# The states' second layer as seven block products on one Trainium2 core

## The chip, the cores and the metric

The kernel runs on one core of a Trainium2 chip. The metric is the device time of one execution in microseconds (us); a time is the median of several runs. A profile is one execution recorded on the chip, with start and length of every instruction. TensorE (PE) does the matmuls, and its weight loads are listed apart as PEld. VectorE (DVE), ScalarE (ACT) and GpSimd (POOL) do the elementwise work. SyncE (SP) issues transfers. PSUM is the memory that TensorE writes its results to[...]; SBUF is the memory for everything else on the core.

## The reference, cut to what matters

An attention between tokens and states comes first, per batch and head; then every token row and every state row, 512 wide with its heads side by side, goes through a gated feed-forward layer. All of it is fp32.

```python
# B, H, S, Ns, D = 8, 8, 512, 32, 64
xread = softmax(scale * x @ state.T) @ state      # (B, H, S, D): tokens
sread = softmax(scale * state @ x.T) @ x          # (B, H, Ns, D): states
attn  = concatenate([xread, sread], axis=2)       # 544 rows per batch
x = attn, heads side by side                      # (8 * 544, 512) = (4352, 512)

h = x @ w_in                                      # w_in  (512, 2048)
g = h * cos(h)
out = g @ w_out                                   # w_out (2048, 512)
```

The tokens are 8 x 512 rows, the states 8 x 32 = 256 rows. The change concerns the last line for those 256 rows. The weights come as fp64 values and are turned into fp32 on the chip from their bits.

## The kernel before

`w_out` lies on chip in four blocks. A row half is 1024 of the 2048 rows (8 tiles of 128, `NH = 8`), a column half 256 of the 512 columns.

```python
w_out = consts.tile([P, 2, NF, HD], F32)          # NF = 16 tiles of 128 rows, HD = 256
a11, a12 = w_out[:, 0, 0:NH], w_out[:, 0, NH:NF]  # first column half
a21, a22 = w_out[:, 1, 0:NH], w_out[:, 1, NH:NF]  # second column half
s1 = consts.tile([P, NH, HD], F32)
s2 = consts.tile([P, NH, HD], F32)
s3 = a21                                          # overwrites a21
s4 = consts.tile([P, NH, HD], F32)
```

The token part takes the batches in pairs. Two batches and two row halves make a 2 x 2 block product. It is done with seven products in place of eight (the Strassen-Winograd scheme). Each uses either a block of the weights or one of four sums of blocks. Those sums are made once, on GpSimd:

```python
block_at = {16: (ALU.add, s1, a21, a22, lo), 18: (ALU.add, s1, a21, a22, hi),
            19: (ALU.subtract, s2, s1, a11, lo), 20: (ALU.subtract, s2, s1, a11, hi),
            21: (ALU.subtract, s4, a12, s2, lo), 22: (ALU.subtract, s4, a12, s2, hi),
            32: (ALU.subtract, s3, a11, a21, lo), 33: (ALU.subtract, s3, a11, a21, hi)}
```

`s3` takes the place of `a21`, which is gone from then on. The last two of a pair's seven products are put off and done beside later tiles, one step (two matmuls of 512 columns) at a time:

```python
class Pair:
    # ...
        self.left = [(p7, i) for i in range(NH)] + [(p4, i) for i in range(NH)]
    def more(self, n):
        for _ in range(n):
            if self.left:
                p, i = self.left.pop(0)
                p(self, i)

def product(bank, w, g, i):
    for ch in range(2):
        nc.tensor.matmul(out=acc[bank][ch], lhsT=w[:, i, P * ch:P * ch + P],
                         rhs=g.g, start=(i == 0), stop=(i == NH - 1))
    return i == NH - 1

def plus(out, bank, ch, b):                       # L630: PSUM to SBUF
    nc.vector.scalar_tensor_tensor(out=out.t[:, ch], in0=acc[bank][ch],
                                   scalar=TWO_PI, in1=b.t[:, ch],
                                   op0=ALU.mult, op1=ALU.add)

def p7(pr, i):
    last = product(SIDE, s3, pr.b[2, i], i)
    free(pr.b[2, i])
    if last:
        for ch in range(2):
            plus(pr.u, SIDE, ch, pr.u)
        total(pr.p5, pr.u, pr.p5)                 # put on the list `later`
        store(2 * pr.n + 1, 1, pr.p5)             # likewise

def p4(pr, i):
    last = product(SIDE, a22, pr.b[1, i], i)
    # ... the same with a store of pr.u
```

The states come last, as 16 tiles of 128 rows of the hidden layer, in the order f = 8 to 15, then 0 to 7. A tile has four matmuls of 256 columns (the 256 states), and a gate `h * cos(h)` of two ScalarE and two VectorE instructions. Two PSUM buffers `h` take turns.

```python
def hidden(t):                                    # L471
    t.hp = hps.tile([P, S], F32, name="h")[:, 0:t.n]
    for i in range(t.kn):                         # 4 for a state tile
        nc.tensor.matmul(out=t.hp, lhsT=t.lhs(i), rhs=t.rhs(i),
                         start=(i == 0), stop=(i == t.kn - 1))

def gate(t):   # ScalarE, L567
def gate2(t):  # VectorE, L570
def gate3(t):  # ScalarE, L573
def gate4(t):  # VectorE, L580: t.g = t.hp * t.q, into a slot of g_all
```

The second layer of the states is a plain product: for each tile two matmuls (states 0 to 127 and 128 to 255) of 512 columns, summed up in two PSUM banks. It needs `a21`, so two quarters of `w_out` are read from memory once more and turned into fp32 again.

```python
loads += [out_load(1, 0), out_load(1, 4)]         # a21 once more
# ...
def state_product(t, i):                          # L748
    nc.tensor.matmul(out=acc[MAIN][i], lhsT=t.g[:, P * i:P * i + P],
                     rhs=w_out[:, :, t.f, :], start=(t.n_th == 0),
                     stop=(t.n_th == NF - 1))

def state_output(t):
    if t.n_th < NF - N_LAST:                      # N_LAST = 3
        for i in range(2):
            state_product(t, i)
        t.last_pair.more(2)                       # two put-off steps of the last pair
        free(t)
        return
    # ... the last three tiles: six products, bank by bank, and state_store(i):
    #     ScalarE takes a bank to SBUF (L771), four transfers of 32 x 512
```

The loop over the tiles gives each engine its instructions in this order. Every engine works through its own in order.

```python
for step, t in enumerate(all_tiles):
    # ...
    hidden(t); gate(t); gate2(t)
    gate3(t)
    if later: later.pop(0)()                      # a total or a store on VectorE
    gate4(t)
    while len(line) >= LAG: output(line.pop(0))   # the tile three steps back
    line.append(t)
for t in line:
    output(t)
while later:
    later.pop(0)()
```

Of the kernel before, what the change touches and what calls it, by code (L numbers as in the profile page):

```python
# [9 lines left out]
F32 = mybir.dt.float32  # L10
I32 = mybir.dt.int32
U32 = mybir.dt.uint32
ALU = mybir.AluOpType
ACTF = mybir.ActivationFunctionType
# [3 lines left out]
TWO_PI = 2.0 * math.pi  # L18
# [3 lines left out]
def kernel(  # L22
# [8 lines left out]
    nc = tc.nc  # L31

    B, H, S, D = x.shape
    Ns = state.shape[2]
    Dm, Dff = moe_w_in.shape
    P = 128
    NK = Dm // P
    NF = Dff // P
    NC = S // P
    T = S + Ns  # L40
    WC = 512
    HS = S // 2
    scale = 1.0 / math.sqrt(D)
# [6 lines left out]
    osb = ctx.enter_context(tc.tile_pool(name="osb", bufs=2))  # L50
# [16 lines left out]
    NH = NF // 2  # L67
    HD = Dm // 2
    w_in = consts.tile([P, NK, Dff], F32)
    w_out = consts.tile([P, 2, NF, HD], F32)  # L70
    a11, a12 = w_out[:, 0, 0:NH], w_out[:, 0, NH:NF]
    a21, a22 = w_out[:, 1, 0:NH], w_out[:, 1, NH:NF]
    s1 = consts.tile([P, NH, HD], F32)
    s2 = consts.tile([P, NH, HD], F32)
    s3 = a21
    s4 = consts.tile([P, NH, HD], F32)

    NG = 28
    g_all = consts.tile([P, NG, S], F32)
    g_free = list(range(NG))  # L80
    xT = consts.tile([P, NK, S], F32)
    x_b = consts.tile([P, NC, H, D], F32)
# [13 lines left out]
    raw_at = [g_all[:, NG - RG * (3 - i):NG - RG * (2 - i)] for i in range(3)]  # L96
    raw_at = [r.rearrange("p t s -> p (t s)") for r in raw_at]
# [28 lines left out]
    def load_state(half, queues):  # L126
        b = slice(4 * half, 4 * half + 4)
        for k in range(NK):
# [10 lines left out]
    at = [aps.tile([P, S], F32, name=f"at{j}") for j in range(2)]  # L139
    acc = [[ops.tile([P, S], F32, name=f"o{m}{ch}") for ch in range(2)]  # L140
           for m in range(2)]
# [14 lines left out]
    f64 = moe_w_in.dtype != F32  # L156
# [9 lines left out]
    def out_load(m, f):  # L166
        return w_out[:, m, f:f + 4], w_out_src[:, m, f:f + 4]
# [6 lines left out]
             out_load(1, 8), out_load(1, 0), out_load(1, 12), out_load(1, 4)]  # L174
    N_LOADS = len(loads)

    loads += [out_load(1, 0), out_load(1, 4)]
    raw_at += [t.rearrange("p a b -> p (a b)")
               for t in (x_b.rearrange("p c h d -> p c (h d)"), xT)]
    raws = {}  # L180
    n_fetched = 0

    def fetch(n):
        nonlocal n_fetched
        while n_fetched < n:
            dst, src = loads[n_fetched]
            if f64:
                m, w = dst.shape[1:]

                at_, c0 = (n_fetched - 2) % 3, 0  # L190
                if n_fetched < 4:
                    at_, c0 = n_fetched // 2, n_fetched % 2 * 2 * m * w
                if n_fetched >= N_LOADS:
                    at_ = 3 + n_fetched - N_LOADS
                raw = raw_at[at_].bitcast(I32)[:, c0:c0 + 2 * m * w]
                raw = raw.rearrange("p (m f) -> p m f", m=m)
                nc.sync.dma_start(out=raw, in_=src.bitcast(I32))
                raws[n_fetched] = raw.rearrange("p m (f w) -> p m f w", w=2)
            else:
                nc.sync.dma_start(out=dst, in_=src)  # L200
            n_fetched += 1
# [374 lines left out]
    def gate4(t):  # L576
        if not hasattr(t, "slot"):
            t.slot = g_free.pop(0)
            t.g = g_all[:, t.slot, 0:t.n]
        nc.vector.tensor_tensor(t.g, t.hp, t.q, op=ALU.mult)  # L580
# [7 lines left out]
    MAIN, SIDE = 0, 1  # L588
# [94 lines left out]
    def free(t):  # L683
        g_free.append(t.slot)
# [56 lines left out]

    N_LAST = 3
    kept_back = []

    def state_product(t, i):
        nc.tensor.matmul(out=acc[MAIN][i], lhsT=t.g[:, P * i:P * i + P],  # L748
                         rhs=w_out[:, :, t.f, :], start=(t.n_th == 0),
                         stop=(t.n_th == NF - 1))  # L750

    def state_output(t):
        if t.n_th < NF - N_LAST:
            for i in range(2):
                state_product(t, i)
            t.last_pair.more(2)
            free(t)
            return
        kept_back.append(t)
        if len(kept_back) == N_LAST:  # L760
            t.last_pair.more(2 * N_LAST)
            for i in range(2):
                for u in kept_back:
                    state_product(u, i)
                state_store(i)

    def state_store(i):
        nb = P // Ns
        rows = out.rearrange("(b t) d -> b t d", t=T)[nb * i:nb * i + nb, S:T]
        ot = osb.tile([P, Dm], F32, name="ot")  # L770
        nc.scalar.activation(ot, acc[MAIN][i], func=ACTF.Copy, scale=TWO_PI)  # L771
        for m in range(nb):
            (nc.sync, nc.scalar)[m % 2].dma_start(
                out=rows[m], in_=ot[Ns * m:Ns * m + Ns, :])

    def tiles():
        pr = None
# [24 lines left out]
    def warm(n, to):  # L802

        for _ in range(n):
            nc.tensor.matmul(out=to, lhsT=zeros[:, 0:P], rhs=zeros, start=True,  # L805
                             stop=True)
# [33 lines left out]
    def plan(b):  # L840
# [69 lines left out]

    conv_at = {s: 4 + i for i, s in enumerate(
        (0, 1, 2, 3, 4, 5, 6, 7, 8, 11, 12, 13, 14, 15))}
    conv_at.update({B * NF + 5: N_LOADS, B * NF + 7: N_LOADS + 1})

    def blocks(op, out_, a, b, r):
        nc.gpsimd.tensor_tensor(out_[:, r], a[:, r], b[:, r], op=op)
# [14 lines left out]
    for step, t in enumerate(all_tiles):  # L931
        s = step % NF
        if s == 0 and t.b < B:
            steps = plan(t.b)
        todo = [p[s] if t.b < B else [] for p in steps]

        def go(n):
            for p in todo[n]:
                part(*p)

        last, conv = conv_at.get(step - 1, -1), conv_at.get(step, -1)
        if step == B * NF + (0 if f64 else 8):
            fetch(N_LOADS + 2)
        if step == 4:
            warm(1, acc[MAIN][0])
        ahead = all_tiles[step + 1:step + 3]
        if seven(t):
            if t.f % 2 == 0:
                hidden_b(t)
                sums_b(t)  # L950
                if s == NF - 2 and seven(all_tiles[step + 2]):
                    halves(t.b + 1)
        elif step != 1:
            hidden(t)
        first = len(ahead) > 1 and seven(ahead[0]) and ahead[0].f % 2 == 0
        if first:
            if not seven(t):

                h = t.hp
                take_slot(t)  # L960
                nc.scalar.copy(t.g, h)
            hidden_a(*ahead)
        if step == 0:
            hidden(all_tiles[1])
            warm(3, acc[MAIN][0])
            gate(t)
            gate2(t)
            convert(3, "bcdf")
            convert(4, "1")
            go(0)  # L970
        else:
            go(0)
            if step == 5:
                states(1, acc[SIDE][1])
            if not (seven(t) and t.f % 2):
                gate(t)
            gate2(t)
            if step == 3:
                warm(4, acc[MAIN][0])
                part(0, "products", 1, SIDE)  # L980
            if first:
                sums_a(ahead[0])
            go(1)
            go(3)
            if step == 1:
                convert(4, "bcdf")
            elif last >= 0:
                convert(last, "bcdf")
            if conv >= 0 and not todo[1]:
                convert(conv, "1")  # L990
        gate3(t)
        if seven(t) and t.f % 2 == 0:
            gate(t.second)
        if step == 3:
            part(0, "products_kept", 1, SIDE)


        full = t.b % 2 == 1 and 1 < t.b < B and NH - 1 <= s < NH + 4
        if later and not full:
            later.pop(0)()  # L1000
        for u, new in zip(all_tiles[step + 2:step + 4], (False, True)):
            if seven(u) and u.f % 2 == 0 and new_pair(u) == new:
                sw_sums(u)
        gate4(t)
        if conv >= 0 and todo[1] and step > 0:
            convert(conv, "1")
        if t.pair is not None:
            sums(t)
        if step == 6:
            states_kept(1, acc[SIDE][1])  # L1010
        go(2)
        if conv >= 0:
            convert(conv, "2")
        go(4)
        for u in all_tiles[step + 5:step + 6]:
            if seven(u) and new_pair(u):
                halves(u.b)
        if step in block_at:
            blocks(*block_at[step])
        if t.pair is not None:  # L1020
            sums2(t)
        while len(line) >= (LAG if step >= 2 * NH else LAG + 1):
            output(line.pop(0))
        line.append(t)
    for t in line:
        output(t)
    while later:
        later.pop(0)()
# [1 line left out]
_INS = ['x', 'state', 'moe_w_in', 'moe_w_out']  # L1030
_OUTS = [((4352, 512), 'float32')]
# [25 lines left out]
```

## Time and profile before

| | us |
|---|---|
| time, median of 3 runs | 763.38 (761.82 to 763.51) |
| span of the profiled execution | 762.9 |
| TensorE busy | 751.9 (99%) |
| VectorE busy | 513.5 (67%) |
| ScalarE busy | 317.8 (42%) |
| GpSimd busy | 261.6 (34%) |
| states' stage, from its first hidden layer | 665.88 to the end |

"Busy" counts the time in which an engine has an instruction under way; the ends of matmuls are modelled, so that the duration of one matmul record overlaps the next record. Lines such as L748 are lines of the kernel before. In a list of groups a line gives the line, the engine, the operation, output and inputs with their shapes and the count, then busy time and the mean of one in ns, then the idle time of the engine ahead of it and what ended that. An arrow `<-` with an engine after an idle time names what was waited for.

### The profile page before, as it was taken

To read this page: it belongs to the slowest core of one execution; us is meant where nothing else is said; L and a number is where in the kernel's file an instruction comes from. 1 tells how busy PE (TensorE), PEld (TensorE's weight loads), DVE (VectorE), ACT (ScalarE), POOL (GpSimd) and SP (SyncE) were. 2 spreads that over 40 slices of the span, in tenths; PEclk is the share of its full clock that TensorE was granted. 3 is DMA by queue.
4 is the path that set the end of the run, shared out by engine and by line. 5 is a ranking of instruction groups with operands and counts; after the bars stand their busy time and mean duration, and the time that the engine had idled before them with its cause. 6 is when DMAs were issued, how large, how long until landed. Compare 5 with 4: busy or idle time off the path is not lost.

```text
span 762.9 us, 8427 instructions
## 1 busy us (share of the span) xinstructions
PE 751.9 (99%) x2880; PEld 381.5 (50%) x2880; DVE 513.5 (67%) x850; ACT 317.8 (42%) x526; POOL 261.6 (34%) x267
## 2 busy tenths in 40 slices
PE   8998999999999999999999999999999999999997
PEld 4443443445555554445555554455555554455554
DVE  4768778746886788846886788747878774432431
ACT  3877943623363435333362336333443334212212
POOL 2344268777121212663121113751211226500200
PEclk9999999999999999999999999999999999999999
DMA  8595471060012510160104310340100110500021
GB/s 247 166 276 173 143 126 29 4 107 1 3 26 36 100 24 9 25 115 0 23 7 86 52 28 1 60 78 1 28 1 2 28 28 1 138 0 15 14 42 41
DMA packets 161962, 43.54 MB, mean 57 GB/s; under 512 B 153920, under 2 KB 153920, under 8 KB 161920
## 3 DMA queue, kind: packets, MB, share of 16 engines
q1 hardware_dynamic: 161024, 42.49, 25.8%
q10 hardware_dynamic: 768, 0.39, 0.2%
q8 instruction: 23, 0.38, 0.2%
q14 instruction: 19, 0.16, 0.1%
q0 software_dynamic: 128, 0.13, 0.1%
HBM read 34.08 MB, written 8.91 MB: 56 GB/s over the span
## 4 chain that ended last, share of the span: by engine, by line
PE 92%; DVE 3%; ACT 2%; DMA 1%; POOL 1%; issue 1%; SPq 0%; DVEq 0%; ACTq 0%; POOLq 0%
PE o L624 50%; PE h L471 15%; PE h L514 14%; PE at L319 5%; PE o L748 4%; PE at L409 2%; PE o L319 1%; PE at L392 1%; DMA x_b<-in_x_dram 1%; DVE w_out L237 0%; ACT q L567 0%; DVE i L333 0%; PE o L805 0%; DVE g_all L580 0%; POOL g_all L586 0%
## 5 line engine op out<-in xcount | busy, mean ns | idle before, releaser
L624 PE MATMUL o<-g_all,w_out 128*128 128x512 f32 x512 | 236.5, 598 | 0.4 <-POOL w_out L242 0.4
L624 PE MATMUL o<-g_all,s 128*128 128x512 f32 x384 | 177.3, 598 | 0.0
L586 POOL TENSOR_TENSOR g_all<-g_all 128x512 f32<-128x512 f32 x89 | 124.8, 1423 | 107.2 <-DVE g_all L580 107.2
L624 PEld LDWEIGHTS o<-g_all,w_out 128*128 128x128 f32 x512 | 93.9, 190 | 113.6 <-issue 108.8
L573 ACT ACTIVATE q<-q,halfpi 128x512 f32<-128x512 f32 (+1 forms) x144 | 101.0, 701 | 90.1 <-DVE q L570 90.0
L570 DVE TENSOR_TENSOR q<-q,h 128x512 f32<-128x512 int32 (+1 forms) x69 | 42.9, 622 | 107.3 <-ACT q L567 107.2
L624 PEld LDWEIGHTS o<-g_all,s 128*128 128x128 f32 x384 | 70.8, 190 | 88.1 <-issue 84.4
L471 PE MATMUL h<-aT,sw 128*128 128x512 f32 x224 | 106.2, 597 | 2.9 <-DVE g_all L580 2.4
L567 ACT ACTIVATE q<-g_all 128x512 int32<-128x512 f32 x75 | 46.9, 625 | 142.2 <-DVE g_all L560 141.8
L567 ACT ACTIVATE q<-h 128x512 int32<-128x512 f32 (+1 forms) x69 | 37.8, 547 | 132.0 <-PE h L471 131.9
L570 DVE TENSOR_TENSOR q<-q,g_all 128x512 f32<-128x512 int32 x75 | 52.9, 705 | 36.1 <-ACT q L567 36.1
L471 PEld LDWEIGHTS h<-aT,sw 128*128 128x128 f32 x224 | 41.9, 190 | 56.6 <-issue 45.7
L509 POOL TENSOR_TENSOR swS<-sw 128x128 f32<-128x128 f32 x35 | 17.6, 503 | 147.6 <-PE h L514 107.2
L580 DVE TENSOR_TENSOR g_all<-g_all,q 128x512 f32<-128x512 f32 x75 | 54.2, 723 | 14.4 <-ACT q L573 14.3
L580 DVE TENSOR_TENSOR g_all<-h,q 128x512 f32<-128x512 f32 (+1 forms) x69 | 42.8, 621 | 22.3 <-ACT q L573 21.4
L242 POOL TENSOR_TENSOR w_out<-w_out,s 128x1024 int32<-128x1024 int32 x10 | 23.9, 2392 | 78.2 <-DVE w_out L237 74.1
L509 POOL TENSOR_TENSOR swS<-sw,swS 128x128 f32<-128x128 f32 x35 | 18.3, 523 | 87.1 <-PE h L514 86.6
L514 PEld LDWEIGHTS h<-aT,sw 128*128 128x128 f32 x144 | 27.4, 190 | 34.4 <-issue 28.5
L514 PE MATMUL h<-aS,sw 128*128 128x256 f32 x144 | 43.1, 381 | 0.1
L514 PE MATMUL h<-aT,sw 128*128 128x256 f32 x144 | 42.8, 379 | 0.0
L514 PE MATMUL h<-aS,swS 128*128 128x256 f32 x144 | 42.8, 379 | 0.0
L242 POOL TENSOR_TENSOR w_in<-w_in,s 128x1024 int32<-128x1024 int32 (+1 forms) x10 | 19.3, 1932 | 37.9 <-DVE w_in L237 22.0
(107 smaller groups left out, 897.1 us busy)
## 6 DMA issues: line engine op xcount, KB each, us to landing
out_dram<-ot SPq DMA_DIRECT2D x132, 64.0 KB, 2.0
g_all<-in_moe_w_out_dram SPq DMA_DIRECT2D x8, 1024.0 KB, 4.9
g_all<-in_moe_w_in_dram SPq DMA_DIRECT2D x6, 1024.0 KB, 5.9
xT<-in_x_dram SPq DMA_DIRECT2D x96, 64.0 KB, 2.3
x_b<-in_x_dram SPq DMA_DIRECT2D x24, 256.0 KB, 4.6
x_b<-in_x_dram SPq DMA_DIRECT2D x16, 128.0 KB, 4.0
g_all<-in_moe_w_in_dram SPq DMA_DIRECT2D x4, 512.0 KB, 6.0
x_b<-in_moe_w_out_dram SPq DMA_DIRECT2D x1, 1024.0 KB, 5.4
```

Of the source, the lines that this page charges most:

```text
L242: nc.gpsimd.tensor_tensor(bits, bits, e, op=ALU.add)
L319: nc.tensor.matmul(out=(to or at)[j][Ns * k:Ns * k + Ns, 0:n], lhsT=w[D * j:D * j + D, self.b, Ns * k:Ns * k + Ns], rhs=r(slice(D * j, D * ...
L471: nc.tensor.matmul(out=t.hp, lhsT=t.lhs(i), rhs=t.rhs(i), start=(i == 0), stop=(i == t.kn - 1))
L509: engine.tensor_tensor(o, x1, x2, op=op)
L514: nc.tensor.matmul(out=out, lhsT=w, rhs=r, start=True, stop=True)
L567: nc.scalar.activation(t.q.bitcast(I32), t.hp, func=ACTF.Copy, bias=0.25)
L570: nc.vector.tensor_tensor(t.q, t.q.bitcast(I32), t.hp, op=ALU.subtract)
L573: nc.scalar.activation(t.q, t.q, func=ACTF.Sin, bias=halfpi, scale=-TWO_PI)
L580: nc.vector.tensor_tensor(t.g, t.hp, t.q, op=ALU.mult)
L586: engine.tensor_tensor(out, a, b, op=ALU.subtract)
L624: nc.tensor.matmul(out=acc[bank][ch], lhsT=w[:, i, P * ch:P * ch + P], rhs=g.g, start=(i == 0), stop=(i == NH - 1))
L748: nc.tensor.matmul(out=acc[MAIN][i], lhsT=t.g[:, P * i:P * i + P], rhs=w_out[:, :, t.f, :], start=(t.n_th == 0), stop=(t.n_th == NF - 1))
```

## The change

The states' second layer is done with the same seven-product scheme. The two blocks of states (columns 0 to 127 and 128 to 255 of `g`) take the part of the two batches of a pair. The weight sums `s1` to `s4`, which the token part has left on chip, are used again, and `a21` isn't needed. The two reads and their conversions fall away. For each pair of tiles f and f + 8, VectorE makes four differences of 128 x 128 blocks, in the free half of the tiles' slots or in place. All products of the second layer stand at the end as one block: seven products of eight matmuls with 256 columns each, in three PSUM banks. Two products are added onto others in the bank itself. The put-off steps of the last pair are given out one for each state tile in place of two, and the results are sent in quarters.

```diff
-    loads += [out_load(1, 0), out_load(1, 4)]
-    raw_at += [t.rearrange("p a b -> p (a b)")
-               for t in (x_b.rearrange("p c h d -> p c (h d)"), xT)]
 # ...
-    def state_product(t, i):
-        nc.tensor.matmul(out=acc[MAIN][i], lhsT=t.g[:, P * i:P * i + P],
-                         rhs=w_out[:, :, t.f, :], start=(t.n_th == 0),
-                         stop=(t.n_th == NF - 1))
+    def state_sums(t):
+        if t.f >= NH:
+            rows_of[t.f] = t
+            return
+        b1 = rows_of[t.f] = t
+        b2 = rows_of[t.f + NH]
+        b1.x = g_all[:, b1.slot, 2 * HR:4 * HR]
+        b2.x = g_all[:, b2.slot, 2 * HR:4 * HR]
+        t1, t2, t4 = b1.x[:, R1], b1.x[:, R2], b2.x[:, R1]
+        for o, x1, x2 in ((t1, b1.g[:, R2], b1.g[:, R1]),
+                          (t2, b2.g[:, R2], t1),
+                          (b1.g[:, R2], b2.g[:, R2], b1.g[:, R2]),
+                          (t4, b2.g[:, R1], t2)):
+            nc.vector.tensor_tensor(o, x1, x2, op=ALU.subtract)

     def state_output(t):
-        if t.n_th < NF - N_LAST:
-            for i in range(2):
-                state_product(t, i)
-            t.last_pair.more(2)
 # ... and the rest of the old one, with state_store
+        t.last_pair.more(1)
+
+    def state_products():
+        x1, x2, x3 = [t[:, 0:HD] for t in (at[0], acc[MAIN][0], acc[MAIN][1])]
+        ots = [osb.tile([P, Dm], F32, name="ot") for _ in range(2)]
 # ... c11, c12, c21, c22: quarters of ots; a, u2, u3: parts of xT
+        def mul(x, w, b, start):
+            for i in range(NH):
+                nc.tensor.matmul(out=x, lhsT=b(i), rhs=w[:, i, :],
+                                 start=(start and i == 0),
+                                 stop=(i == NH - 1), skip_group_check=True)
 # ... plus: VectorE, o = TWO_PI * x + b;  keep: ScalarE, o = TWO_PI * x
 # ... send: four transfers of 32 x 256, two on each of two queues
+        mul(x1, a11, lambda i: rows_of[i].g[:, R1], True)
+        keep(a, x1)
+        mul(x2, s2, lambda i: rows_of[i].x[:, R2], True)
+        plus(u2, x2, a)
+        mul(x1, a12, lambda i: rows_of[i + NH].g[:, R1], False)
+        keep(c11, x1)
+        send(0, 0, c11)
+        mul(x3, s1, lambda i: rows_of[i].x[:, R1], True)
+        plus(u3, x3, a)
+        mul(x2, s3, lambda i: rows_of[i].g[:, R2], False)
+        plus(c22, x2, u3)
+        send(1, 1, c22)
+        mul(x3, s4, lambda i: rows_of[i + NH].g[:, R2], False)
+        plus(c12, x3, u2)
+        send(1, 0, c12)
+        mul(x2, a22, lambda i: rows_of[i + NH].x[:, R1], False)
+        plus(c21, x2, a)
+        send(0, 1, c21)
 # ... in the loop over the tiles
         gate4(t)
+        if t.pair is None:
+            state_sums(t)
 # ... after it
     while later:
         later.pop(0)()
+    state_products()
```

More of the change, by code (lines that the diff above doesn't have):

```diff
@@ L192, in fetch @@
                     at_, c0 = n_fetched // 2, n_fetched % 2 * 2 * m * w
-                if n_fetched >= N_LOADS:
-                    at_ = 3 + n_fetched - N_LOADS
                 raw = raw_at[at_].bitcast(I32)[:, c0:c0 + 2 * m * w]
@@ L739, in output @@
                 store(2 * pr.n + 1, 0, o)
-    N_LAST = 3
-    kept_back = []
-    def state_product(t, i):
-        nc.tensor.matmul(out=acc[MAIN][i], lhsT=t.g[:, P * i:P * i + P],
-                         rhs=w_out[:, :, t.f, :], start=(t.n_th == 0),
-                         stop=(t.n_th == NF - 1))
-    def state_output(t):
-        if t.n_th < NF - N_LAST:
-            for i in range(2):
-                state_product(t, i)
-            t.last_pair.more(2)
[L757 to L774, printed above, removed]
+    HR = P
+    R1, R2 = slice(0, HR), slice(HR, 2 * HR)
+    rows_of = {}
+    def state_sums(t):
[12 more added lines that the diff above has]
+            nc.vector.tensor_tensor(o, x1, x2, op=ALU.subtract)
@@ new lines, in state_output, with plus, keep, send @@
+    def state_output(t):
+        t.last_pair.more(1)
+    def state_products():
+        x1, x2, x3 = [t[:, 0:HD] for t in (at[0], acc[MAIN][0],
+                                           acc[MAIN][1])]
+        ots = [osb.tile([P, Dm], F32, name="ot") for _ in range(2)]
+        c11, c12 = [ot[:, 0:HD] for ot in ots]
+        c21, c22 = [ot[:, HD:Dm] for ot in ots]
+        a, u2, u3 = [xT[:, i, 0:HD] for i in range(3)]
+        def mul(x, w, b, start):
[3 more added lines that the diff above has]
+                                 stop=(i == NH - 1), skip_group_check=True)
+        def plus(o, x, b):
+            nc.vector.scalar_tensor_tensor(out=o, in0=x, scalar=TWO_PI,
+                                           in1=b, op0=ALU.mult, op1=ALU.add)
+        def keep(o, x):
+            nc.scalar.activation(o, x, func=ACTF.Copy, scale=TWO_PI)
+        def send(i, m, src):
+            nb = P // Ns
+            rows = out.rearrange("(b t) d -> b t d", t=T)[nb * i:nb * i + nb,
+                                                          S:T]
+            for n in range(nb):
+                (nc.sync, nc.scalar)[n % 2].dma_start(
+                    out=rows[n, :, HD * m:HD * m + HD],
+                    in_=src[Ns * n:Ns * n + Ns, :])
+        mul(x1, a11, lambda i: rows_of[i].g[:, R1], True)
[16 more added lines that the diff above has]
+        send(0, 1, c21)
@@ L912 @@
         (0, 1, 2, 3, 4, 5, 6, 7, 8, 11, 12, 13, 14, 15))}
-    conv_at.update({B * NF + 5: N_LOADS, B * NF + 7: N_LOADS + 1})
     def blocks(op, out_, a, b, r):
@@ L941 @@
         last, conv = conv_at.get(step - 1, -1), conv_at.get(step, -1)
-        if step == B * NF + (0 if f64 else 8):
-            fetch(N_LOADS + 2)
         if step == 4:
```

## The prediction

> **What bounds the kernel now.** I began with the page of the kernel before: the busy times, then the 40 slices.
>
> ```profile
> PE 751.9 (99%) x2880; PEld 381.5 (50%) x2880; DVE 513.5 (67%) x850; ACT 317.8 (42%) x526; POOL 261.6 (34%) x267
> PE   8998999999999999999999999999999999999997
> PEclk9999999999999999999999999999999999999999
> ```
>
> TensorE is busy 99% of the span with a granted clock of nine tenths or more in every slice. No other engine is over 67%. Only the first slice and the last have room on TensorE. The chain that ended last, by line, says the same:
>
> ```profile
> PE 92%; DVE 3%; ACT 2%; DMA 1%; POOL 1%; issue 1%; SPq 0%; DVEq 0%; ACTq 0%; POOLq 0%
> PE o L624 50%; PE h L471 15%; PE h L514 14%; PE at L319 5%; PE o L748 4%; PE at L409 2%; PE o L319 1%; PE at L392 1%; DMA x_b<-in_x_dram 1%; DVE w_out L237 0%; ACT q L567 0%; DVE i L333 0%; PE o L805 0%; DVE g_all L580 0%; POOL g_all L586 0%
> ```
>
> The part that the change touches is L748 (the states' second layer), 4%. Next I read that chain in order of time for the states' stage, which runs from 665.9 us to the end (columns: start us, us, what):
>
> ```profile
> 731.39 1.72 PE o L748 x4
> 733.10 3.43 PE o L624 x8
> 736.54 1.73 PE h L471 x8
> 738.26 1.72 PE o L748 x4
> 739.98 1.73 PE h L471 x8
> ...
> 750.31 1.73 PE h L471 x8
> 752.04 6.88 PE o L748 x16
> 758.92 0.02 issue
> 758.94 0.60 ACT ot L771
> ```
>
> Each fp32 matmul of the code is two records here: L748 is called 32 times in the code and the list of groups has 64 records of it. Pieces touch without a gap, so the cadence can be read off: a record of 512 columns takes 6.88/16 = 0.430 us, one of 256 columns (L471 in this stage) 1.73/8 = 0.216 us. The mean durations in the list of groups (592 and 379 ns) overlap one another and must not be multiplied by counts. The stage windows show that this holds throughout:
>
> ```profile
> 690.00:738.00 48.00, 48.00 (x141) 26.49 (x140) 16.43 (x29) 10.19 (x18) 4.99 (x2) 1.00 0.14 23
> 738.00:759.00 21.00, 20.90 (x66) 12.04 (x64) 5.43 (x12) 5.13 (x12) 0.00 (x0) 1.00 0.21 37
> ```
>
> The columns are the length, then busy time of PE, PEld, DVE, ACT and POOL, the clock, the DMA share and GB/s. TensorE is busy 48.00 of 48.00 us while the reloaded weights are converted (the 4.99 on POOL are two conversion adds). What the other engines and the transfers do there costs no time now.
>
> [...] 0.216/0.430 = 0.502. [...] loads take 190 ns each, and 256-column records with a load apiece still follow each other at 216 ns. [...] the dependent sums of L509 on VectorE, which have 0.0 us idle before the second:
>
> ```profile
> L509 DVE TENSOR_TENSOR swS<-sw 128x128 f32<-128x128 f32 x1 | 0.3, 291 | 0.8 <-ACT sw L445 0.8
> L509 DVE TENSOR_TENSOR swS<-swS,sw 128x128 f32<-128x128 f32 x1 | 0.3, 291 | 0.0
> L630 DVE SCALAR_TENSOR_TENSOR held<-o,held 128x512 f32<-128x512 f32 x40 | 25.3, 677 | 3.4 <-PE o L624 3.3
> ```
>
> **The change part by part.**
>
> *Removed from TensorE:* 32 matmuls of 512 columns, 64 records x 0.430 = 27.5 us, all on the path.
>
> *Added to TensorE:* 7 products x 8 row blocks = 56 matmuls of 256 columns, 112 records x 0.216 = 24.2 us, all on the path. The shapes (128x128 weights, 256 moving columns) are those of L471 in this stage. Net -3.3 us: one product of eight. It is not more because the reload was never on the path.
>
> *Removed elsewhere:* two reads of 1 MB; two conversions with two ScalarE operations (1.16 and 1.14 us), two VectorE ones (0.69 and 1.23 us) and one on GpSimd (2.49 us) each. They lie beside a TensorE that is busy 48.00 of 48.00 us. Worth 0.
>
> *Moved:* the 16 leftover products of the last pair (p7 and p4, two matmuls each) now go one per state tile, three of them after the last tile, where before two went with each tile for eight tiles. The same count of records, so TensorE's work is unchanged. A state tile takes 1.73 + 1.72 = 3.45 us throughout, which is the rhythm of the kernel before after 738.26. That stretch shows that ScalarE and VectorE keep up with it. The kernel before has these instructions for one of its tiles:
>
> ```profile
> 748.69 0.39 ACT L567 ACTIVATE q<-h 128x256 int32<-128x256 f32 x1 [2.06 <-PE h L471]
> 749.11 0.42 DVE L570 TENSOR_TENSOR q<-q,h 128x256 f32<-128x256 int32 x1 [2.02 <-ACT q L567]
> 749.56 0.51 ACT L573 ACTIVATE q<-q,halfpi 128x256 f32<-128x256 f32 x1 [0.49 <-DVE q L570]
> 750.11 0.43 DVE L580 TENSOR_TENSOR g_all<-h,q 128x256 f32<-128x256 f32 x1 [0.58 <-ACT q L573]
> ```
>
> The hidden layer of that tile ended at 748.59, so the gate is through at 750.54, 1.95 us later. Its PSUM buffer is wanted again after 1.72 + 1.73 + 1.72 = 5.17 us. No wait there.
>
> *Added to VectorE:* four 128x128 subtractions on each of the last eight tiles, 4 x 0.29 = 1.16 us per tile, 9.3 us in all, less 3.8 us of removed conversions. They follow the gate: 1.95 + 1.16 = 3.11 us after the hidden layer, within the 3.45 us of a tile. They matter once. The eighth p7 product falls on the eleventh tile, and VectorE, in order, empties its two banks only after that tile's four subtractions. Then the first p4 product must start in the same bank. VectorE finishes the first bank at 3.11 + 0.69 = 3.80 us, TensorE asks for it at 1.72 + 1.73 = 3.45 us: **a stall of about 0.35 us**. The second bank is ready at 4.49 us and asked for at 3.80 + 0.86 = 4.66, so nothing is added.
>
> *The block at the end:* the last tile's sums are ready 3.11 us after its hidden layer, and three p4 products (5.15 us) come before the block, so its start is covered. Three accumulators serve seven products, and between the last write of one and the next write into it there is always another product of 16 x 0.216 = 3.45 us. An eviction of 128x256 takes about 0.42 us (an estimate from the 256-column VectorE rows). Every hand-over inside is hidden. The output buffers wait for the last pair's stores, which should be issued within some 6 us of the block's start (two store steps on VectorE and eight issues at about 0.43 us, the ScalarE queue's pace at the end) and take 2.0 us to land by the page; the first is wanted after three products, 10.4 us.
>
> *The tail:* before, 762.9 - 758.92 = 4.0 us pass from the last record to the end, 0.60 of them in the 128x512 eviction. After, one 128x256 eviction on VectorE, 0.42 us, and four transfers of half the size. About -0.2 us.
>
> Sum: -27.5 + 24.2 + 0.35 - 0.2 = **-3.2 us**, so 763.38 - 3.2 = 760.2. I put the median at 760.1, as the first of these numbers is 0.5 us over the profiled span and may be a little high.
>
> **The rivals.**
> 1. *Small matmuls cost by their own durations.* If 112 x 0.379 us counted against 64 x 0.592, the change would lose 42.4 - 37.9 = 4.5 us, giving 768. Against it: the start-to-start cadence above. For it: in the kernel before, 256-column records run in uninterrupted groups of eight only, and the block has 112 in a row, so a limit that builds up over a longer run would not be visible yet.
> 2. *The block is serial.* All second-layer work is now at the end, with nothing else for TensorE to do, and each product hangs on an eviction. If six hand-overs each showed about 0.5 us, the saving would be gone: 763. Against it: the order of the products leaves 3.45 us for each.
> 3. *VectorE becomes the bound of the last eight tiles.* Per tile 0.42 + 0.42 + 1.16 + up to 0.69 for a store step is 2.7 of 3.45 us. Every tile could slip a little if the subtractions ran at 0.5 us. Eight slips of 0.3 us give 762.5.
> 4. *The reload was costly after all*, by contention. Then more than 3.3 us comes back, perhaps 758. The windows with TensorE at 100% speak against it.
>
> **Range and chances.** The sure term is 3.3 us, 0.4% of the time. The corrections are a few tenths. The runs before spread over 1.7 us (761.82 to 763.51), which is most of the uncertainty: 758.6 to 761.5. A change of 2% is 15 us, half of all that the states' second layer costs; no step above and no rival comes near it, so within 2% has 0.98.
>
> **What would show it right or wrong.** The seven products fill about 24.2 us without idle time; from the first hidden layer of the states to TensorE's last record some 3.0 us less than 758.92 - 665.9 = 93.0 us; one wait of TensorE on VectorE's L630 eviction, near 0.35 us, in the eleventh state tile; the stages before 665.9 unchanged. The prediction is wrong if 256-column records in the block come more than 0.22 us apart, if gaps stand between the products, or if the state tiles come more than 3.45 us apart.

## The result, and the profile after

The changed kernel takes 759.77 us (median of 4 runs, 758.54 to 760.41), the kernel before 762.71 us (4 runs, 761.82 to 763.51). The ratio is 0.9959, 95% interval 0.9945 to 0.9973. The prediction was 760.1 us, in a range of 758.6 to 761.5. It holds, and so do its larger terms. Two small terms were mis-sized, the one wait of TensorE and the end of the kernel.

First the page of the changed kernel: busy times, and the chain that ended last by line (L619 answers to L624 of the kernel before, L466 to L471, L772 is the new block):

```profile
PE 747.9 (99%) x2928; PEld 389.7 (51%) x2928; DVE 519.9 (69%) x883; ACT 313.2 (41%) x522; POOL 256.6 (34%) x265
PE o L619 51%; PE h L466 15%; PE h L509 14%; PE at L314 5%; PE o L772 2%; PE at L404 2%; PE o L314 1%; PE at L772 1%; PE at L387 1%; DMA x_b<-in_x_dram 1%; ACT q L568 0%; DVE i L328 0%; ACT q L562 0%; PE o L840 0%; POOL g_all L581 0%
```

TensorE is still the bound. It has 48 records more (112 - 64) and 4.0 us less busy time, 3.0 us of it in the states' stage (93.02 to 90.00). The end of the same chain in order of time (start us, us, what):

```profile
723.32 6.87 PE o L619 x16
730.18 3.45 PE at L772 x16
733.63 3.45 PE o L772 x16
737.09 3.45 PE at L772 x16
740.54 13.83 PE o L772 x64
754.37 0.02 issue
754.39 0.42 DVE ot L777
```

The seven products follow one another without a gap, 3.45 us for each 16 records, 0.216 us a record. The stage windows of the changed kernel show the two parts of the states' stage (length, then busy PE, PEld, DVE, ACT, POOL):

```profile
679.60:730.00 50.40, 50.13 (x169) 31.80 (x168) 26.50 (x71) 11.61 (x26) 0.00 (x0) 1.00 0.14 22
730.00:754.30 24.30, 24.30 (x113) 21.09 (x111) 3.65 (x8) 0.77 (x2) 0.00 (x0) 1.00 0.20 38
```

The block is full. In the tiles ahead of it 0.27 us are missing, all of them at one place. The list of waits of TensorE in this stage has one entry (total, times, longest):

```profile
PE o L619 <- DVE held L625: 0.3, 1, 0.3
```

The chain shows where it is:

```profile
703.83 1.74 PE h L466 x8
...
707.60 0.30 DVE g_all L757
707.90 0.02 issue
707.92 0.69 DVE g_all L757 x3
708.62 0.61 DVE held L625
709.23 0.04 issue
709.27 1.98 PE o L619 x4
```

This is the eleventh tile: the hidden layer, its gate (cut), the four differences (L757), and only then the eviction of the finished p7 bank (L625, which reads 128x512 fp32 from PSUM, 0.68 us by its record), on which TensorE waits. From the hidden layer of the next tile, at 707.11, to the one after it, at 711.10, pass 3.98 us, where the other tiles from the fourth on take 3.44: the wait costs 0.54 us, more than the idle time alone.

Executions differ by some 1.5 us for reasons that lie ahead of the states' stage: in the profiles of this study the stage begins anywhere between 662.8 and 665.9 us, with the same code up to there. Of the 1.8 us between the two profiles, 1.1 have arisen by 22 us: from 7.7 to 11.2 us the profile of the kernel before has a granted clock of 0.51, and that of the changed kernel 1.00. The rest arises at about 57 to 60 us. So the experiments are read mainly by two lengths that leave this out: the *stage*, from the start of the states' first hidden layer to the end of TensorE's last record, and the *end*, from there to the end of the span (with the spans to a hundredth: 762.91 before, 758.05 changed).

| kernel | stage | end |
|---|---|---|
| before | 93.02 | 4.01 |
| before, no reload | 93.02 | 4.15 |
| before, no reload, put-off steps spread | 93.02 | 8.48 |
| the same, stores first | 93.02 | 6.09 |
| before, products in halves | 93.18 | 4.01 |
| changed | 90.27 | 3.69 |
| changed, again | 90.27 | 3.70 |
| changed, differences late | 89.73 | 3.70 |
| the same, again | 89.73 | 3.68 |
| changed, hand-overs laid open | 93.44 | 3.69 |
| differences late, sends of 64 rows | 89.73 | 6.88 |
| differences late, sends on three queues | 89.73 | 4.32 |

The change takes 2.75 us from the stage and 0.32 us from the end, 3.07 together; the medians differ by 2.94. Of the 4.9 us between the two profiled spans, the other 1.8 lie ahead of the stage and are none of the change's doing.

### The profile page after: what moved, and what is told of

Read it like the earlier page. It is cut to its first block, busy times and chain, and to the rows that moved or that the text cites. A ratio compares the mean times of both kernels' runs of the same rounds, so it can differ in the third digit from the quotient of the medians.

```text
span 758.0 us, 8557 instructions
## 1 busy us (share of the span) xinstructions
PE 747.9 (99%) x2928; PEld 389.7 (51%) x2928; DVE 519.9 (69%) x883; ACT 313.2 (41%) x522; POOL 256.6 (34%) x265
## 4 chain that ended last, share of the span: by engine, by line
PE 92%; DVE 3%; ACT 1%; DMA 1%; POOL 1%; issue 1%; SPq 0%; DVEq 0%; ACTq 0%; POOLq 0%
PE o L619 51%; PE h L466 15%; PE h L509 14%; PE at L314 5%; PE o L772 2%; PE at L404 2%; PE o L314 1%; PE at L772 1%; PE at L387 1%; DMA x_b<-in_x_dram 1%; ACT q L568 0%; DVE i L328 0%; ACT q L562 0%; PE o L840 0%; POOL g_all L581 0%
## 5 line engine op out<-in xcount | busy, mean ns | idle before, releaser
L619 PE MATMUL o<-g_all,w_out 128*128 128x512 f32 x512 | 237.4, 599 | 0.6 <-POOL w_out L237 0.3
L619 PE MATMUL o<-g_all,s 128*128 128x512 f32 x384 | 177.3, 598 | 0.0
L619 PEld LDWEIGHTS o<-g_all,w_out 128*128 128x128 f32 x512 | 93.8, 190 | 108.6 <-issue 102.6
L619 PEld LDWEIGHTS o<-g_all,s 128*128 128x128 f32 x384 | 70.8, 190 | 88.1 <-issue 84.4
L466 PE MATMUL h<-aT,sw 128*128 128x512 f32 x224 | 106.4, 598 | 2.9 <-DVE g_all L575 2.4
L466 PEld LDWEIGHTS h<-aT,sw 128*128 128x128 f32 x224 | 41.9, 190 | 56.6 <-issue 45.7
L509 PEld LDWEIGHTS h<-aT,sw 128*128 128x128 f32 x144 | 27.4, 190 | 34.4 <-issue 28.5
L509 PE MATMUL h<-aS,sw 128*128 128x256 f32 x144 | 43.1, 381 | 0.1
L509 PE MATMUL h<-aT,sw 128*128 128x256 f32 x144 | 42.8, 379 | 0.0
L509 PE MATMUL h<-aS,swS 128*128 128x256 f32 x144 | 42.8, 379 | 0.0
L466 PE MATMUL h<-st_all,w_in 128*128 128x256 f32 x128 | 30.2, 379 | 0.0
```

The lines of the kernel that those rows point to most:

```text
L466: nc.tensor.matmul(out=t.hp, lhsT=t.lhs(i), rhs=t.rhs(i), start=(i == 0), stop=(i == t.kn - 1))
L509: nc.tensor.matmul(out=out, lhsT=w, rhs=r, start=True, stop=True)
```

## The experiments

**The reload alone.**

```diff
-    loads += [out_load(1, 0), out_load(1, 4)]
...
-    conv_at.update({B * NF + 5: N_LOADS, B * NF + 7: N_LOADS + 1})
...
-        if step == B * NF + (0 if f64 else 8):
-            fetch(N_LOADS + 2)
```

> The kernel before, with the two repeated reads of weights and their conversions left out and nothing else changed (the states' second layer then uses the weight sum that lies in that place, so its results are not the reference's). Theory: the reload lay beside a TensorE that was never idle, so the states' stage, from the start of its first hidden layer to TensorE's last record, stays at 93.0 us, and the time is that of the kernel before within 0.2%. Rival (the reload cost time by contention, and part of the 2.9 us comes from there): the stage gets 0.5 to 3 us shorter.

Measured: stage 93.02 us, as before; 763.3 us (12 runs) against 762.86, ratio 1.0008 (1.0000 to 1.0017). Two megabytes read a second time and 13.4 us of conversion on three engines were worth nothing, as they lay beside a full TensorE. That no weights are reloaded says what the change does, not where its time comes from.

**The put-off steps alone.** With the reload in place they can't be spread, since the reloaded `a21` overwrites the `s3` that p7 reads; so this is built on the run above.

```diff
-            t.last_pair.more(2)
+            t.last_pair.more(1)
...
-            t.last_pair.more(2 * N_LAST)
+            t.last_pair.more(N_LAST)
```

> As the run without the reload, and the put-off steps of the last pair given out one for each state tile, as in the changed kernel; the second layer stays a plain product beside the tiles. Theory: moving the steps costs nothing by itself, stage 93.0 us, no wait of TensorE at the change from p7 to p4, because no differences stand ahead of the eviction on VectorE. Rival (the denser tiles make the gate late, or the wait comes from the move itself): a wait of TensorE of 0.3 us or more at one or several tiles, stage 93.4 us or more.

Measured: stage 93.02 us and no wait of TensorE, so the theory holds for the stage. But the time was 767.35 us (one run), 4.5 us over the kernel before, which neither side had expected. All of it is after TensorE's last record. The end of this kernel's chain:

```profile
757.05 0.61 ACT ot L770
...
758.09 2.02 DMA out_dram<-ot
...
760.33 0.71 DVE ot L654
```

The last pair's two stores now come due at the very end. Their steps on VectorE (L654) need the output buffers that the states' evictions (L770) and their transfers hold. The second starts at 760.33 us, and four transfers are still to come after it.

**The same with the stores first.**

```diff
+            while later:
+                later.pop(0)()
             for i in range(2):
                 for u in kept_back:
                     state_product(u, i)
                 state_store(i)
```

> The run with the spread put-off steps and without the reload, with the last pair's stores made ahead of the last products of the states and not behind them. Theory: the 8.5 us that passed there from TensorE's last record to the end came from the stores, whose two steps on VectorE stood behind the states' evictions in the two output buffers; with the stores first they lie partly beside the last 5.2 us of products, and the states' evictions wait for the buffers instead: 5 to 7 us from the last record to the end. So in the changed kernel it is the block of 24 us that covers the stores. Rival (only the order was at fault): back to 4.0 us.

Measured: end 6.09 us, stage 93.02, 765.21 us (one run). The order was half of it, the missing cover the other half: there are 16 transfers for the end, and 5.2 us of products hide only some of them. The chain shows what the states' second eviction now waits for, an output buffer of the stores: their last issues on SyncE, the transfer, then the eviction.

```profile
756.65 0.51 SPq L660
757.15 0.04 issue
757.20 2.02 DMA out_dram<-ot
...
759.32 0.60 ACT ot L772
```

In the changed kernel the same stores run beside the block of 24 us, and its end is 3.69 us. So spreading the steps needs the products at the end; with the plain product beside the tiles, the spread loses 4.5 us, more than the eighth product gains, and still 2.1 us with the stores first. The reverse, the block at the end without the spread, was not run.

**Shorter matmuls alone.**

```diff
-        nc.tensor.matmul(out=acc[MAIN][i], lhsT=t.g[:, P * i:P * i + P],
-                         rhs=w_out[:, :, t.f, :], start=(t.n_th == 0),
-                         stop=(t.n_th == NF - 1))
+        for m in range(2):
+            nc.tensor.matmul(out=acc[MAIN][i][:, HD * m:HD * m + HD],
+                             lhsT=t.g[:, P * i:P * i + P],
+                             rhs=w_out[:, m, t.f, :],
+                             start=(t.n_th == 0 and m == 0),
+                             stop=(t.n_th == NF - 1), skip_group_check=True)
```

> The kernel before, with each 512-column matmul of the states' second layer cut into two of 256 columns: the same product, 64 matmuls in place of 32. Theory: columns are what counts, 128 records x 0.216 = 27.6 us in place of 64 x 0.430 = 27.5, stage 93.1 to 93.2 us; so the whole gain of the changed kernel's products is the eighth that is left out. Rival (each matmul has a fixed cost of its own, which the changed kernel pays on 56 in place of 32): the stage grows by a visible amount, 1 us or more; then fewer, wider products would gain more.

Measured: stage 93.18 us, 0.16 more, for 64 more records and 64 more weight loads: 2.5 ns each. The kernel before would gain nothing from smaller matmuls, and the change loses next to nothing by them. What it gains on TensorE is the eighth product.

**The one wait.**

```diff
         gate4(t)
-        if t.pair is None:
-            state_sums(t)
...
             output(line.pop(0))
+        if t.pair is None:
+            state_sums(t)
         line.append(t)
```

> The changed kernel, with the four differences of a state tile put behind the steps that follow it in VectorE's order (in the same loop turn, but after the eviction of a finished put-off product). Theory: the one wait of TensorE in the states' stage, 0.54 us longer than a normal tile at the eleventh, came from the differences standing ahead of the eviction of p7; it goes away, the stage falls from 90.3 to 89.75 us, and the time falls by about 0.5 us (0.07%, at the edge of what can be told from the times). Rival (the eviction itself is late, or the differences now delay the gates of the next tile enough to hold TensorE): the stage stays at 90.3 us or grows.

Measured: stage 89.73 us, 0.54 less, and 759.47 us (5 runs), ratio 0.9965 (0.9951 to 0.9979). A second time, beside the changed kernel on one chip:

> The changed kernel itself, timed beside the next run on the same chip. Theory: ratio to the kernel before 0.9955 to 0.9965 (2.8 us from the stage and 0.35 us from the end), stage 90.3 us. Rival (part of the first comparison was the difference between executions, as the first hidden layer of the states came 1.8 us earlier in that profile although nothing ahead of it had changed): a ratio above 0.997.

> The changed kernel with the differences behind the eviction, a second time, to set its time beside the changed kernel's on the same chip. Theory: 0.55 us under the changed kernel, ratio lower by 0.0007; stage 89.7 us with no wait at the change from p7 to p4. Rival (what the stage gains is lost at the end or ahead of it): the two ratios the same or in the other order.

Measured: the changed kernel 759.84 us (5 runs), ratio 0.9957 (0.9944 to 0.9969), and with the late differences 758.11 us (5 runs), ratio 0.9943 (0.9930 to 0.9955). The stages are 90.27 and 89.73 us, as in the first pair. TensorE at the change from p7 to p4 with the late differences (start us, us, operation):

```profile
704.29 1.88 PE L619 MATMUL o<-g_all,w_out 128*128 128x512 f32 x4
706.01 1.89 PE L466 MATMUL h<-st_all,w_in 128*128 128x256 f32 x8
707.73 1.88 PE L619 MATMUL o<-g_all,w_out 128*128 128x512 f32 x4
```

Pieces 1.72 us apart: no wait. In the profile of the first pair VectorE has the two evictions at 706.18 us and the differences behind them at 707.38; in the changed kernel the differences stand at 707.60 and the evictions at 708.54. So the differences in front of the eviction were its cause. The stage says 0.54 us, twice; the medians can't tell the two kernels apart, as their intervals overlap. The 1.7 us between the last two medians is not the edit's either: it is mostly a different mix of executions with a mean granted clock of 0.999 or more (two of five against four of five). Among those alone the mean times differ by 0.4 us, among the others by 0.5. As far as the traces go, this is the version that beats both: 3.3 us of stage under the kernel before.

**The hand-overs.** The seven products in an order in which each bank is written again right after it was read (arguments and sends are left out):

```diff
         mul(x1, a11, ...); keep(a, x1)
-        mul(x2, s2, ...);  plus(u2, x2, a)
         mul(x1, a12, ...); keep(c11, x1)
         mul(x3, s1, ...);  plus(u3, x3, a)
-        mul(x2, s3, ...);  plus(c22, x2, u3)
-        mul(x3, s4, ...);  plus(c12, x3, u2)
+        mul(x3, s4, ...)
+        mul(x2, s2, ...);  plus(u2, x2, a);  plus(c12, x3, u2)
+        mul(x2, s3, ...);  plus(c22, x2, u3)
         mul(x2, a22, ...); plus(c21, x2, a)
```

> The changed kernel with its seven products in an order in which a product comes straight after the one whose accumulator it adds onto: a11 and a12, s1 and s4, s2 and s3 and a22, so that four hand-overs of a bank (matmul to eviction to matmul) have nothing in between. The same matmuls and evictions. Theory: in the changed kernel all hand-overs are hidden by the 3.45 us of the product in between, and each that is laid open costs an eviction of 0.38 to 0.42 us and some 0.15 us of hand-over and restart: block 24.35 + 4 x 0.57 = 26.6 us, four waits of TensorE of about 0.45 us. Rival (the hand-overs already cost something in the order of the changed kernel, or the accumulator is not what TensorE waits for): the block stays within 1 us of 24.35.

Measured: stage 93.44 us, the block 27.50 us where the changed kernel has 24.34, 764.5 us in one run. The block of this kernel begins on TensorE so:

```profile
731.54 3.62 PE L772 MATMUL at<-w_out,g_all 128*128 128x256 f32 x16
735.63 3.72 PE L772 MATMUL at<-w_out,g_all 128*128 128x256 f32 x16 [0.47 <-ACT xT L781]
739.18 3.62 PE L772 MATMUL o<-s,g_all 128*128 128x256 f32 x16
```

The first hand-over costs 735.63 - 731.54 - 3.45 = 0.64 us before the next record, and the product after it takes 3.55 in place of 3.45. Four of them cost 3.16 us, 0.79 each: nearly the whole 3.3 us of the eighth product. The direction was the theory's, the size was not (0.57 was expected). In an undisturbed run a record starts 0.16 us before the modelled end of the one ahead of it. Here the eviction starts 0.02 us after that end (735.19 against 735.17 us in the chain), and the estimate had left the 0.16 us out. The 0.15 us that it had for hand-over and restart are there: 0.02 us ahead of the eviction, 0.04 us behind it, and the 0.10 us of the longer product.

**The end of the kernel.** Two tries to shorten it, both on top of the late differences. First, transfers of 64 rows:

```diff
-            for n in range(nb):
-                (nc.sync, nc.scalar)[n % 2].dma_start(
-                    out=rows[n, :, HD * m:HD * m + HD],
-                    in_=src[Ns * n:Ns * n + Ns, :])
+            for n in range(0, nb, 2):
+                (nc.sync, nc.scalar)[n // 2].dma_start(
+                    out=rows[n:n + 2, :, HD * m:HD * m + HD],
+                    in_=src[Ns * n:Ns * n + 2 * Ns, :])
```

> The changed kernel with two edits: the four differences of a state tile behind the eviction of a finished put-off product, as in the run before, and the results of each quarter sent as one transfer of 64 rows on each of two queues, in place of two of 32 rows each. Theory: the first edit takes 0.55 us from the stage (89.7 us); of the second, the last transfer starts one issue of 0.43 us earlier, and the time from TensorE's last record to the end falls from 3.6 to about 3.2 us. Together 0.9 to 1.0 us under the changed kernel, ratio to the kernel before 0.9945 to 0.9955. Rival (a transfer of twice the size takes as much longer as its issue is earlier): from the last record to the end stays at 3.6 us.

Measured: the stage is 89.73 us as expected, but the end 6.88 us, and the time 762.58 us (13 runs), ratio 0.9995 (0.9987 to 1.0003). Neither side had this: the theory expected a shorter end, the rival the same one. The mean busy share of the 16 transfer engines in tenths, from the last sends on, 40 slices of this kernel's 753.4 to 760 us:

```profile
DMA  1111111111011011101111111111100000000000
```

and of the changed kernel's 754.8 to 758 us:

```profile
DMA  0000000000255772356661000000000000000000
```

The four transfers of 32 rows keep up to 7 tenths of the engines busy and are through in less than 1 us. With 64 rows the share is one tenth for some 5 us. The packets of the same two windows, the 64-row kernel first:

```profile
DMA packets 203, 0.20 MB, mean 30 GB/s; under 512 B 8, under 2 KB 203, under 8 KB 203
DMA packets 192, 0.13 MB, mean 41 GB/s; under 512 B 64, under 2 KB 192, under 8 KB 192
```

A row is one packet of 1 KB. The last quarter has 128 rows, so 67 of the 195 such packets in the first window belong to the quarter before: its send was still under way when the last one was issued at 753.5 us. The queues show the order, SyncE's as q1 and ScalarE's as q10. From 753.4 to 756 us:

```profile
q10 hardware_dynamic: 66, 0.07, 7.1%
q1 hardware_dynamic: 41, 0.04, 6.4%
```

and from 753.4 to 760 us:

```profile
q10 hardware_dynamic: 132, 0.13, 5.6%
q1 hardware_dynamic: 71, 0.07, 4.3%
```

Up to 756 us ScalarE's queue starts 66 packets, a whole send (64 rows and 2 small packets), which is that of the quarter before; the 66 of its last send all come later. SyncE's starts 41 of its 71, the first few of them also from the quarter before. The small packets (under 512 B) are 2 for each transfer of 64 rows (8 for four) and 16 for each of 32 rows (64 for four).

The shares of the queues give an estimate of how many packets are under way at a time. With 64 rows, 9.9% of 16 engines' 6.6 us is 10.5 us of packet time, in the 5.1 us of the slices that are not empty: about two. With 32 rows, 15.1% (7.6 and 7.5 by the same view) of 16 engines' 3.2 us is 7.7 us, in 0.96 us: about eight. Why a transfer of 64 rows has fewer under way was not shown; the trace does not number the engines. So two things go with the long end: few packets at a time, and sends, one every 3.45 us, that are made while the one before is still under way. No run tells the two apart.

Second, the last four transfers with their 32 rows on three queues:

```diff
+                q = (nc.sync, nc.scalar)[n % 2]
+                if (i, m) == (0, 1):
+                    q = (nc.sync, nc.scalar, nc.gpsimd, nc.gpsimd)[n]
```

> The changed kernel with the differences behind the eviction, and the four transfers of the last quarter spread over three queues (SyncE, ScalarE one each, GpSimd two) in place of two on each of two queues; the transfers keep their size of 32 rows. Theory: [...] with 32 rows each the transfers stay fast, and the end comes after 3.2 to 3.7 us, depending on how fast GpSimd issues. Rival (GpSimd's own issue is slower than SyncE's second): 3.8 us or more from TensorE's last record to the end.

Measured: end 4.32 us, 0.6 more than with two queues, as the rival had it; 758.89 us (6 runs), ratio 0.9959 (0.9946 to 0.9971). GpSimd's issues in the timeline:

```profile
753.28 1.03 POOL L791 DMA_DIRECT2D out_dram<-ot  x2 [87.73 <-DVE ot L777]
```

It issues both between 753.28 and 754.31 us, while SyncE's single one was out at 753.32. The last issue is out 1.33 us after the last eviction, where ScalarE's pair in the changed kernel needs 0.89 us: 0.4 of the 0.6 us. The two queues of the changed kernel stay the better choice.

## Why the prediction was right, point by point

- **What bounds the kernel.** As read, with one slip: the slices show room on TensorE in the fourth as well as in the first and the last (8, 8 and 7 tenths). Nothing rests on it.
- **Products.** The sum had 112 records at 0.216 us for the block, 24.2 us; the seven products start 3.453 us apart, 24.17 us in all. The cadence of groups of eight holds over 112 records in a row, so the first rival falls by the trace, and the halved products show the same inside the kernel before.
- **The reload, worth 0.** Shown by the run without it. The fourth rival falls.
- **The moved steps.** TensorE's work is unchanged and the gates keep up, as written. That it "is unchanged" in time is true only with the block behind it. The prediction had the stores in its working, as something whose buffers the block must wait for, and had not seen that without the block they would lie open at the end.
- **The stall of about 0.35 us.** Right place, right cause, shown by the run with the late differences; the size was 0.54. The step "VectorE finishes the first bank at 3.80 us, TensorE asks for it at 3.45" counted both from the modelled end of the hidden layer, 705.57 us. VectorE was done 3.66 us later (709.23), a little sooner than written, since the four differences took 1.02 us in a row and not 1.16. But a next record starts 0.16 us ahead of the modelled end, so TensorE would have gone on 3.27 us after it, at 707.11 + 1.73 = 708.84. The wait to 709.27 is 0.44 us (from the unrounded starts), and the four records after it take 1.82 us in place of 1.72. That last 0.10 had no term in the sum.
- **The block's hand-overs, all hidden.** No gap in the trace. The run that lays four open has 0.79 us for each, so the second rival is the right account of another order of the products. The 3.45 us between the uses of a bank are more than four times those 0.79 us.
- **VectorE as the bound (third rival).** It holds TensorE up in no tile but that one. The four differences take 1.02 us, but not evenly: in all eight tiles the second, which reads the result of the first, starts 0.33 us after it, and the third and the fourth 0.21 and 0.20 us after the one ahead, before that one's 0.29 us are over. So the 0.0 us ahead of the second L509, which the prediction shows, is a rounding: there too the second starts 0.33 us after the first, at 0.29 us each. For these subtractions a wait for the result just ahead does cost time: 0.03 us between the two, and an overlap of 0.08 us that is lost.
- **The end, -0.2 us.** It was -0.32. The eviction fell from 0.60 to 0.42 us as written. The other 0.14 us lie behind it. The last transfers, half as large, landed in 1.5 and 1.7 us (medians on SyncE's and ScalarE's queue) where the kernel before has 1.7 and 2.0; the sum had put nothing down for that.

The two errors, +0.19 and -0.12 us, nearly cancel, and that is luck. The sum was -3.2, stage and end together give -3.07. The starting point, 763.38, was the median of three runs; a fourth brought it to 762.71, and from there the sum leads to 759.5 (759.77 measured). Both lie well inside a range of 2.9 us, whose width comes from the spread of the executions and not from the terms.

## What to carry to other kernels

Here TensorE was full from start to end (99% busy), and the change was worth what it took from TensorE's own stream: one block product of eight, and nothing of 2 MB of transfers and their conversion (stage 93.02 us with and without them). What was lost was in the order: a bank that was written again straight after it was read cost 0.79 us each time, and four differences in front of an eviction in VectorE's order cost TensorE 0.54 us. Put the late work of an earlier stage where a long run of matmuls still follows: with the block of 24 us behind it the end was 3.69 us here, without it 8.48. And when the end of a transfer is on the path, measure it in more than one shape: four transfers of 32 rows kept the end at 3.7 us here, two of 64 rows over 2 batches made it 6.88.

## What the runs showed that I had not expected

- The matmuls that waited for a bank cost more than the wait. In the stall of the changed kernel the weight load was not made ahead during the wait: it starts at 709.27 us together with the matmul, after 0.68 us of idle time of its own put down to the same eviction. The first record after the wait then takes 0.70 us in place of 0.59. In the run with open hand-overs the load starts at 735.62 us and the matmul at 735.63, and the product takes the same 0.10 us more.
- Four 128-column subtractions on VectorE take 1.02 us in a row, while one alone is listed with 288 ns: the two that don't read the result just ahead overlap it by 0.08 us.
- The results of a quarter sent as two transfers of 64 KB, each over 2 batches x 32 rows in memory, gave an end of 6.88 us; sent as four of 32 KB they gave 3.68 to 3.70.
